# lam loaded as one row, the set-up reordered, and the first weight slice gated on the second q pair

## Chip, cores and metric

One core of one Trainium2 chip. The metric is device time of one execution in microseconds (us); the kernel before is given by the median of 11 executions.

## What is computed

Two steps. The first is a causal linear attention with decay over q, k and v of shape (4 batches, 8 heads, 768 positions, 64), cut into blocks of 64 in the reference; `lam` holds one decay factor per head (8 numbers in all). The second takes its output as 3072 tokens of 512 and runs them through two weight matrices with an activation between them.

```
per block, per batch and head:
  intra = ((qb @ kb.T) * Dmask) @ vb            # Dmask[i,j] = lam**(i-j) for i >= j, else 0
  inter = (qb * lam**(pos+1)) @ kv_state
  out   = intra + inter
  kv_state = lam**64 * kv_state + (kb * lam**(63-pos)).T @ vb
x = out as (tokens, heads*dim)                   # 3072 x 512
h = x @ w_in                                     # 512 -> 2048
g = h where h >= 1, 0 where h <= -1, else (h+1)**2 / 4
y = g @ w_out                                    # 2048 -> 512, float32
```

## The kernel before

**Tiling.** The attention runs over 24 chunks of 128 positions (6 to a batch). Powers of `lam` are put into q and k by elementwise products with tables, so a chunk needs only a triangular mask, not the full decay matrix. The feed-forward runs over 6 stages of 512 tokens, so four chunks of attention feed one stage. Chunks 0 and 1 are loaded as a pair in an even/odd layout (`PF = (0,)`), and take their own paths (`f_sp`, `f_op`).

**One chunk.** q, k and v are loaded in float32 by SyncE (SP). VectorE or GpSimd multiplies q and k by the tables and casts them to bf16 (`cast_q` L289, `cast` L284); ScalarE casts v into a block layout `vi` whose other half must be zero (L320). TensorE transposes q and k (L332, L325), which VectorE or ScalarE copy to SBUF (`kT` L342, `kbd` L335 for chunks 2 and 3, `qT` L338). TensorE then makes the scores (L390 for the first pair, L380 for chunks 2 and 3, L398 later), VectorE masks them (L405, L408, L410), TensorE adds the state's product and the scores' product with v into `po` (L425, L428; L440, L446 for the first pair) and updates the state in PSUM (L365, L369), from which ScalarE copies the diagonal blocks into `ubd` (L373). ScalarE copies `po` to `xT` (L458). The zero halves of `vi`, `kbd` and `ubd` are written once, in the set-up.

**Feed-forward.** `xT` times `w_in` (L470), ScalarE's relu (L479), three VectorE steps (L489, L495, L500), `gT` times `w_out` (L518), a ScalarE copy (L523), a store. `w_in` and `w_out` come in four slices each, through GpSimd's DMA queue with a cast to bf16 (L188, L192).

**Set-up (L105 to L156).** ScalarE loads its function table and issues the load of `lam` as a broadcast to all 128 partitions. GpSimd makes an identity matrix, two tables of positions (`pos_i`), and two masks, and zeroes two of the four `vi`; VectorE zeroes the other buffers. ScalarE takes Ln of `lam`, VectorE multiplies it by the positions (`arg`), and ScalarE's Exp of that gives `tab_q`, `tab_p` and `tab_k`.

**What sets the order.** Scheduling is manual: a planner written into the kernel (`run_plan`, L217) runs a small list simulation with a time for each operation, a due time worked back from TensorE's later work, and a model of the loads (`FIRST_BYTE` L212, L256 to L262), and then emits the operations in the order of the simulated starts. Each engine executes its own operations in that order, and waits in it. So the numbers of the model change the order of the program and nothing else. The loads and weight slices follow `ORDER` (L67): chunks 0 to 3, the four w_in slices, chunk 4, two w_out slices, chunk 5, two w_out slices, then chunks 6 and up. `LORD` gives the order of q, k and v (0, 1, 2) within a chunk. `GATE` (L72) makes a load or slice wait for the landing of another; without an entry, a chunk behind slices waits for the last slice but one, and the first w_out slice behind chunk 4 waits for the last w_in slice. `W_AFTER` (L215) puts slices behind the second q pair's casts on GpSimd. A load that waits holds all later loads on SP; a slice that waits holds GpSimd's later casts.

Of the kernel before, what the change touches and what calls it, by code (L numbers as in the profile page):

```python
# [8 lines left out]
F32 = mybir.dt.float32  # L9
# [14 lines left out]
def kernel(  # L24
# [44 lines left out]
    D0 = (8350, 11900, 15450, 19000)  # L69
    FIRST = [(0, 2), (2, 4)]  # L70
    L0 = [(0, 0), (0, 1), (1, 0), (1, 1), (0, 2), (1, 2), (0, 3), (1, 3)]
    GATE = {(0, 0): ("ld", 2, 1)}  # L72
    LORD = {0: (0, 1, 2), 2: (1, 0, 2)}
    DBG = False

    const = ctx.enter_context(tc.tile_pool(name="const", bufs=1))
# [26 lines left out]
    SYNC = mybir.DependencyInfo(mybir.DependencyClass.Sync, mybir.DependencyReason.DATA)  # L103

    nc.scalar.preload_act_table_set("natural_log_exp_and_others")  # L105
    lam_b = const.tile([128, H], F32)
    nc.scalar.dma_start(out=lam_b, in_=lam.partition_broadcast(128))


    ident = const.tile([128, 128], BF16)  # L110
    make_identity(nc, ident)
    pos_i = const.tile([128, 2, NCB], I32)
    nc.gpsimd.iota(pos_i[:, 0], pattern=[[C, NCB]], base=-S // 2, channel_multiplier=1)
    nc.gpsimd.iota(pos_i[:, 1], pattern=[[1, 2], [2 * C, NCB // 2]], base=-S // 2, channel_multiplier=2)
    causal = const.tile([128, 128], F32)
    nc.gpsimd.memset(causal, 1.0)
    nc.gpsimd.affine_select(
        out=causal, in_=causal, compare_op=AX.is_ge, fill=0.0,
        base=0, pattern=[[1, 2], [2, 64]], channel_multiplier=-1)
    causal2 = const.tile([128, 2, 128], F32)  # L120
    nc.gpsimd.memset(causal2, 1.0)
    for e in range(2):
        for rows, base in ((slice(0, 128), 128 - e), (slice(0, 64), -e)):
            nc.gpsimd.affine_select(
                out=causal2[rows, e], in_=causal2[rows, e], compare_op=AX.is_ge, fill=0.0,
                base=base, pattern=[[1, 2], [2, 64]], channel_multiplier=-2)


    NKB, NUB, NV = 3 if len(PF) < 2 else 0, 3, 4
    kbd = [const.tile([128, HP, 2, 128], BF16, name=f"kbd{i}") for i in range(NKB)]  # L130
    ubd = [const.tile([128, HP, 128], BF16, name=f"ubd{i}") for i in range(NUB)]
    vi = [const.tile([128, HP, 2, 2, D], BF16, name=f"vi{i}") for i in range(NV)]
    one = const.tile([128, 1], F32)
    nc.vector.memset(one, 1.0)
    for t in vi[:2] + kbd[:2] + ubd[:1]:
        nc.vector.memset(t, 0.0)
    for t in vi[2:]:
        nc.gpsimd.memset(t, 0.0)
    pos = const.tile([128, 2, NCB], F32)
    nc.scalar.copy(pos, pos_i)  # L140
    for t in kbd[2:] + ubd[1:]:
        nc.vector.memset(t, 0.0)
    ln_lam = const.tile([128, H], F32)
    nc.scalar.activation(out=ln_lam, in_=lam_b, func=AF.Ln)
    arg = const.tile([128, 2, NCB, H], F32)
    nc.vector.tensor_tensor(arg.rearrange("p a c h -> p (a c) h"), _bc(pos.rearrange("p a c -> p (a c)"), 2, H),
                            _bc(ln_lam, 1, 2 * NCB), op=AX.mult)
    tab_q = const.tile([128, 2, NCB // 2, H], F32)
    nc.scalar.activation(out=tab_q.rearrange("p a c h -> p (a c) h"), in_=arg[:, 1], func=AF.Exp)
    tab_p = const.tile([128, 2, 2, H], F32)  # L150
# [1 line left out]
                         in_=arg[:, 1].rearrange("p (e m) h -> p e (m h)", e=2)[:, :, :2 * H], func=AF.Exp, scale=-1.0)  # L152
    tab_k = const.tile([128, NCB, H], F32)
    nc.scalar.activation(out=tab_k, in_=arg[:, 0], func=AF.Exp, scale=-1.0)
    tab_qn = const.tile([128, NCB, H], F32)
    causal_n = const.tile([128, 128], F32)  # L156

# [51 lines left out]
        ops.append(OPS[key])  # L209

    MMS, FETCH = {"s": 8, "o": 12}, 1300
    FIRST_BYTE = 2950  # L212
    LDD, QXD, KXD, STD = 20000, 7000, 7000, 3000
    ON_POOL, ON_DVE = (1,), ((0, 1),)
    W_AFTER = {1: ("cq", 1, 1), 2: ("cq", 1, 1)}  # L215

    def run_plan(free):  # L217

        users = {x.key: [] for x in ops}
        for x in ops:  # L220
            x.needs = [OPS[y] for y in x.keys if y in OPS]
            for y in x.needs:
                users[y.key].append(x)
        left = {x.key: len(x.needs) for x in ops}
        topo = [x for x in ops if not x.needs]
        for x in topo:
            for u in users[x.key]:
                left[u.key] -= 1
                if left[u.key] == 0:
                    topo.append(u)  # L230
        assert len(topo) == len(ops)
        for x in reversed(topo):
            d = [u.due - u.ns - x.extra - LAT for u in users[x.key] if not u.dma]
            x.due = min(d + ([x.own] if x.own is not None else []), default=1e9)
            if x.dma or x.key[0] in ("l1", "l2"):
                x.due = x.own
        left = {x.key: len(x.needs) for x in ops}
        ready = {e: [] for e in free}
        for x in topo:
            if not x.needs:  # L240
                ready[x.eng].append((0, x))
        out_seq, xfer, dma_free, fetched = [], [0] * RING, FIRST_BYTE, 0
        while len(out_seq) < len(ops):
            t, e = min((max(free[e], min(r for r, _ in lst), xfer[-RING] if e == "SP" else 0), e)
                       for e, lst in ready.items() if lst)
            r, x = min(((r, x) for r, x in ready[e] if r <= t), key=lambda p: (p[1].due, p[0]))
            ready[e].remove((r, x))
            ns = x.ns + (720 if x.perf and free["POOL"] > t else 0)
            free[e] = t + ns
            x.t, x.end = t, t + ns + x.extra  # L250
            if e == "PE":
                n = fetched + 2 * MMS.get(x.key, MMS.get(x.key[0], 4))
                if n // 256 > fetched // 256:
                    dma_free = max(dma_free, t) + FETCH
                fetched = n
            if x.dma:  # L256
                dma_free = max(dma_free, t + (1300 if e == "SP" else 2100)) + x.dma
                x.end = dma_free + 1400
                if x.key[0] in ("ld", "lq") and x.key[1] >= (FAR if x.key[0] == "ld" else FAR // 2):
                    x.end += SLACK if (x.key[1] if x.key[0] == "ld" else 2 * x.key[1]) >= 10 else NEAR  # L260
                if e == "SP":
                    xfer.append(dma_free)  # L262
            out_seq.append((t, len(out_seq), x))
            for u in users[x.key]:
                left[u.key] -= 1
                if left[u.key] == 0:
                    ready[u.eng].append((max(y.t if y.eng == u.eng and y.key != u.gate else y.end + (XSL if u.eng == "SP" and y.eng == "POOL" and u.dma in (640, 1280) else LAT) for y in u.needs), u))
        for t, _, x in sorted(out_seq, key=lambda p: p[:2]):
            if DBG:
                print(f"{t / 1e3:9.3f} {x.due / 1e3:9.3f} {x.eng:5s} {x.ns:6.0f} {x.key}")  # L270
            x.fn()
# [83 lines left out]
    def last_of(a):  # L355

        return a | 1 if a // 2 in PF else a
# [257 lines left out]
    for it in order:  # L615
        if isinstance(it, tuple):
            prev = order[order.index(it) - 1]
            gated = GATE.get(it, len(w_seen) - 1 - prev % 2 if w_seen and isinstance(prev, int) else None)
            need = [("w",) + w_seen[-1], W_AFTER.get(len(w_seen))] if w_seen else []
            key = None  # L620
            if gated is not None:
                key = gated if isinstance(gated, tuple) else ("w",) + w_seen[gated]
                need.append(key)
            add(("w",) + it, "POOL", 900, lambda it=it, wait=gated: f_w(it, wait), need, due=pos_ * 1e-3,
                dma=2560)
            if key is not None:
                OPS[("w",) + it].gate = key
            w_seen.append(it)
            pos_ += 1
            continue  # L630
# [13 lines left out]
            pos_ += 1  # L644
        last_c = it

    for c in range(NCH):
        od, cb = o_due(c) - (DLEAD if c >= DX else 0), c % NCB
        lastu = c - 1 if cb else c - 2
# [28 lines left out]
        if CPS <= c < XT or pf:  # L678
            add(("kT", c), "DVE", 450, lambda c=c: f_kT(c), [("t", c), ("m", c - NQT, 1)])
        for hi in range(2 if c < CPS and not pf else 0):  # L680
            add(("kb", c, hi), "DVE", 365, lambda c=c, hi=hi: f_kb(c, hi), [("t", c), ("s", c - NKB, 1)])
        if cb < NCB - 1:
            add(("u", c), "PE", mm(*[128] * (8 if pf else 4)) + 100 * pf, lambda c=c: f_u(c),
                [("cast", last_of(c), 1), ("cast", last_of(c), 2), ("ub", lastu, 0), ("ub", lastu, 1), ("u", lastu)], due=od - 4000, extra=FILL)
            for hi in range(2):
                add(("ub", c, hi), "ACT", 372, lambda c=c, hi=hi: f_ub(c, hi), [("u", c), ("o", last_of(c - NUB + 1))])
        if pf:
            add(("s", c, 0), "PE", mm(*[128] * 4) + 250, lambda c=c: f_sp(c),
                [("kT", c), ("qT", m, 0), ("qT", m, 1), ("m", c - 2, 0), ("m", c - 2, 1), ("m", c - 1, 0), ("x", 1) if c == 3 else None], due=od - 2500, extra=FILL)
# [7 lines left out]
            add(("m", c, h), "DVE", 690, lambda c=c, h=h: f_m(c, h), [("s", c, h if c < CPS and not pf else 0), ("o", last_of(c - 3)), ("m", c, 0) if h else None])  # L697
        if pf:
            if c % 2:
                add(("o", c), "PE", mm(*[128] * (20 if c == 1 else 24)) + 250, lambda m=m: f_op(m),  # L700
                    [("m", c, 1), ("cast", c, 2), ("ub", c - 1, 0), ("ub", c - 1, 1), ("ub", c - 2, 0), ("ub", c - 2, 1),
                     ("x", c - 3), ("x", c - 2), ("kT", c), ("m", c - 1, 1)], due=od, extra=FILL)
        else:
# [54 lines left out]
            add(("y", y), "ACT", 600, lambda a=(s, ms): f_y(*a), [("l2", n2), ("y", y - 1), ("st", y - NO)])  # L758
            add(("st", y), "SP", 550, lambda a=(s, ms): f_st(*a), [("y", y), ("st", y - 1)], due=st_due(y), dma=780)

    run_plan({"PE": 5500, "ACT": 5600, "DVE": 5000, "POOL": 5000, "SP": 800})


# [28 lines left out]
```

## Time and profile before

| | us |
|---|---|
| median of 11 executions | 221.49 (219.71 to 222.27) |
| the profiled execution | 220.75 |
| its span | 219.0 |
| TensorE matmuls busy | 203.4 |
| first matmul | 8.07 |
| first matmul with w_in | 20.49 |
| first matmul with w_out | 37.56 |

The profile is of one execution; its times count from the start of the span. PE is TensorE, DVE VectorE, ACT ScalarE, POOL GpSimd; a row that begins with time, duration, engine and line is from the timeline, and the bracket at its end says how long the engine had been idle and what released it. SPq, ACTq and POOLq rows are the issue of a DMA, not its transfer. In the DMA view, q1 carries the loads that SP issues, q10 the one of ScalarE (`lam`), and q0 the weight slices of GpSimd.

### The profile page before, as it was taken

How to read it: one execution, taken by the hardware profiler on the slowest of the kernel's cores; microseconds unless marked ns; L12 is line 12 of the kernel's file. 1: busy time of each engine (PE TensorE's matmuls, PEld its weight loads, DVE VectorE, ACT ScalarE, POOL GpSimd, SP SyncE). 2: the span in 40 equal slices, each digit the busy share in tenths (PEclk: the TensorE clock that was granted, in tenths of full speed). 3: DMA queues.
4: the chain of work that ended last, by engine and by line, in shares of the span. 5: the costliest groups of instructions: out<-in, count | busy, mean ns of one | idle time of the engine just before them, and what ended most of it. 6: DMA issues, size and time to landing. Idle time of an engine off the chain costs nothing.

```text
span 219.0 us, 4453 instructions
## 1 busy us (share of the span) xinstructions
PE 203.4 (93%) x1776; PEld 132.9 (61%) x1800; DVE 137.3 (63%) x216; ACT 122.9 (56%) x220; POOL 63.0 (29%) x71
## 2 busy tenths in 40 slices
PE   0399799999999999999999999999999999999994
PEld 0278688685747977777766676744545444444442
DVE  6384588779544697979855967631697655554301
ACT  3347678454836757576648667545765534455030
POOL 8571094227524242812322800342100000000000
PEclk9999999999999999999999999999999999999998
DMA  4999999999999999999999727989785211110122
GB/s 111 278 223 217 200 224 200 185 226 233 157 226 140 243 156 226 168 192 230 200 236 186 151 48 157 198 196 218 245 147 168 62 37 48 48 48 0 51 96 96
DMA packets 96116, 35.42 MB, mean 162 GB/s; under 512 B 78560, under 2 KB 93152, under 8 KB 96096
## 3 DMA queue, kind: packets, MB, share of 16 engines
q1 hardware_dynamic: 91728, 30.94, 67.5%
q0 software_dynamic: 4224, 4.19, 11.8%
q8 instruction: 14, 0.23, 0.4%
q14 instruction: 6, 0.05, 0.1%
q10 hardware_dynamic: 144, 0.00, 0.0%
HBM read 27.27 MB, written 6.29 MB: 153 GB/s over the span
## 4 chain that ended last, share of the span: by engine, by line
PE 91%; DMA 3%; ACT 2%; issue 1%; DVE 1%; POOL 1%; POOLq 0%
PE ph L470 39%; PE py L518 36%; PE ps L398 3%; PE po L428 3%; DMA x0f<-in_q_dram 3%; PE pu L369 2%; PE py L512 1%; PE po L425 1%; PE pt L325 1%; PE py L332 1%; PE pu L365 1%; PE po L420 1%; PE po L446 1%; ACT xT L458 1%; PE po L417 1%
## 5 line engine op out<-in xcount | busy, mean ns | idle before, releaser
L470 PE MATMUL ph<-xT,w_in_sb 128*128 128x256 bf16 (+2 forms) x763 | 95.7, 272 | 1.7 <-ACT xT L458 1.2
L479 ACT ACTIVATE r<-ph,one 128x512 bf16<-128x512 f32 x96 | 65.9, 688 | 48.8 <-PE ph L470 31.9
L518 PE MATMUL py<-w_out_sb,gT 128*128 128x512 bf16 x349 | 86.5, 379 | 1.2 <-issue 0.3
L470 PEld LDWEIGHTS <-w_in_sb 128*128 128x128 bf16 x768 | 63.3, 98 | 24.7 <-issue 1.9
L518 PEld LDWEIGHTS <-gT 128*128 128x128 bf16 x368 | 34.8, 98 | 34.8
L489 DVE TENSOR_SCALAR t<-r 128x1024 bf16<-128x1024 bf16 x48 | 24.4, 509 | 39.6 <-ACT r L479 39.6
L495 DVE TENSOR_TENSOR w<-r,t 128x1024 bf16<-128x1024 bf16 x48 | 38.3, 799 | 1.5
L500 DVE TENSOR_TENSOR gT<-w,t 128x1024 bf16<-128x1024 bf16 x48 | 36.8, 766 | 1.5
L287 POOL TENSOR_TENSOR ks<-x1f,tab_k 128x512 bf16<-128x512 f32 x20 | 23.5, 1175 | 33.3 <-DMA x1f<-in_k_dram 20.7
L523 ACT COPY osb<-py 128x512 f32<-128x512 f32 x23 | 13.5, 585 | 17.9 <-PE py L518 16.6
L296 POOL TENSOR_TENSOR qs<-x0f,tab_q 128x512 bf16<-128x512 f32 x15 | 17.8, 1203 | 18.0 <-DMA x0f<-in_q_dram 13.3
L373 ACT CAST ubd<-pu 64x256 bf16<-64x256 f32 x40 | 14.6, 364 | 6.8 <-PE pu L369 3.7
L294 POOL TENSOR_TENSOR qs<-x0f,tab_qn 128x512 bf16<-128x512 f32 x8 | 9.3, 1161 | 27.1 <-DMA x0f<-in_q_dram 23.6
L410 DVE TENSOR_TENSOR sc<-ps,causal 128x512 bf16<-128x512 f32 x12 | 8.2, 686 | 9.0 <-PE pt L398 8.9
L458 ACT CAST xT<-po 128x512 bf16<-128x512 f32 x15 | 8.8, 584 | 8.3 <-PE po L428 5.1
L428 PE MATMUL po<-sc,vi 128*128 128x128 bf16 x112 | 10.5, 219 | 0.0
L332 PE MATMUL py<-ident,qs 128*128 128x128 bf16 x16 | 2.4, 306 | 8.7 <-POOL qs L296 8.1
L428 PEld LDWEIGHTS <-vi 128*128 128x128 bf16 x112 | 8.4, 98 | 1.0
L425 PE MATMUL po<-qT,ubd 128*128 128x128 bf16 x48 | 8.7, 219 | 0.0
L410 DVE TENSOR_TENSOR sc<-ps,causal_n 128x512 bf16<-128x512 f32 x8 | 5.5, 690 | 5.0 <-PE pt L398 5.0
L320 ACT CAST vi<-x2f 128x512 bf16<-128x512 f32 x14 | 8.5, 615 | 0.0
L410 DVE TENSOR_TENSOR sc<-pt,causal 128x512 bf16<-128x512 f32 x12 | 8.2, 680 | 0.0
(84 smaller groups left out, 132.1 us busy)
## 6 DMA issues: line engine op xcount, KB each, us to landing
out_dram<-osb SPq DMA_DIRECT2D x23, 256.0 KB, 2.5
x1f<-in_k_dram SPq DMA_DIRECT2D x22, 256.0 KB, 4.8
x2f<-in_v_dram SPq DMA_DIRECT2D x22, 256.0 KB, 5.0
x0f<-in_q_dram SPq DMA_DIRECT2D x8, 512.0 KB, 5.4
w_in_sb<-in_moe_w_in_dram POOLq DMA_DIRECT2D x4, 512.0 KB, 7.7
w_out_sb<-in_moe_w_out_dram POOLq DMA_DIRECT2D x4, 512.0 KB, 8.5
x0f<-in_q_dram SPq DMA_DIRECT2D x8, 256.0 KB, 4.1
raw<-in_k_dram SPq DMA_DIRECT2D x1, 512.0 KB, 6.8
```

Source lines behind the costliest of these rows:

```text
L287: eng.tensor_tensor(ks[c], qkv_ld[c, 1], _bc(tab, 2, D), op=AX.mult)
L296: eng.tensor_tensor(qs[m, e], qkv_ld[m, 0][:, :, e], _bc(tab_q[:, e, m % (NCB // 2), :], 2, D), op=AX.mult)
L373: nc.scalar.copy(out=ubd[c % NUB][HD[hi], :, HD[hi]], in_=pu[0][HD[hi], :, HD[hi]])
L410: nc.vector.tensor_tensor(sc_sb[c][:, g], pst[c, g], _bc(causal if c < DX else causal_n, 1, HP), op=AX.mult)
L428: nc.tensor.matmul(po[:, hp], lhsT=vi[c % NV][:, hp, hi].rearrange("p a d -> p (a d)"), rhs=sc_sb[c][:, hi, hp, :], start=(cb == 0 and hi ...
L470: nc.tensor.matmul(ph[:, j * m:(j + 1) * m], lhsT=w_in_sb[:, ko, (ni + j) * 128:(ni + j + 1) * 128], rhs=xT[s][:, ko, tok], start=(ko == 0 ...
L479: nc.scalar.activation(out=o, in_=x, func=AF.Relu, bias=one[:, 0:1])
L489: nc.vector.tensor_scalar(t, r, 0.5, 1.0, op0=AX.mult, op1=AX.min)
L495: nc.vector.tensor_tensor(w, r, t, op=AX.subtract)
L500: nc.vector.tensor_tensor(gT[s][:, f - RW * n:f, tok].rearrange("p (a b) m -> p a b m", a=RW), w.rearrange("p a (b m) -> p a b m", m=m), t ...
L518: nc.tensor.matmul(py_t[s, ms], lhsT=gT[s][:, ko, ms * 128:(ms + 1) * 128], rhs=w_out_sb[:, ko, :], start=(ko == 0), stop=(ko == FO - 1))
L523: nc.scalar.copy(out=osb[s, ms], in_=py_t[s, ms])
```

## The change

`lam` is loaded as one row of 8 numbers into one partition. Ln is taken there; the result is split into three bf16 pieces by VectorE (five operations on 1x8), and TensorE multiplies a row of ones by each piece and adds them up in PSUM (three matmuls), which gives the logarithm on all partitions. GpSimd makes the positions first. Two of the four `vi` are zeroed by ScalarE copies of zeroed ones. `kbd` has two buffers instead of three; they and the third `ubd` are zeroed by planned VectorE operations ("z") after chunk 0's k cast.

In the order of loads, chunk 2 takes q, k, v instead of k, q, v; the first w_in slice waits for the second q pair's landing instead of chunk 2's k; chunk 4's loads wait for the second w_in slice instead of the third, and chunk 6's for the second w_out slice instead of the third. The third slice's own tie to the q casts is dropped (it stays behind the second slice, which has it). The planner's model of loads and of some costs takes other numbers.

```diff
-    GATE = {(0, 0): ("ld", 2, 1)}
-    LORD = {0: (0, 1, 2), 2: (1, 0, 2)}
+    GATE = {(0, 0): ("lq", 1), 4: 1, 6: 5}
+    LORD = {0: (0, 1, 2), 2: (0, 1, 2)}
...
-    lam_b = const.tile([128, H], F32)
-    nc.scalar.dma_start(out=lam_b, in_=lam.partition_broadcast(128))
-    ident = const.tile([128, 128], BF16)
-    make_identity(nc, ident)
+    lam_r = const.tile([1, H], F32)
+    nc.scalar.dma_start(out=lam_r, in_=lam.rearrange("(o h) -> o h", o=1))
     pos_i = const.tile([128, 2, NCB], I32)
...
+    ident = const.tile([128, 128], BF16)
+    make_identity(nc, ident)
...
-    NKB, NUB, NV = 3 if len(PF) < 2 else 0, 3, 4
+    NKB, NUB, NV = 2, 3, 4
...
-    for t in vi[:2] + kbd[:2] + ubd[:1]:
+    ones = const.tile([1, 128], BF16)
+    nc.vector.memset(ones, 1.0)
+    for t in vi[:2]:
         nc.vector.memset(t, 0.0)
-    for t in vi[2:]:
-        nc.gpsimd.memset(t, 0.0)
+    rest = const.tile([1, 3, H], F32)
+    nc.scalar.activation(out=rest[:, 0], in_=lam_r, func=AF.Ln)
     pos = const.tile([128, 2, NCB], F32)
     nc.scalar.copy(pos, pos_i)
-    for t in kbd[2:] + ubd[1:]:
-        nc.vector.memset(t, 0.0)
-    ln_lam = const.tile([128, H], F32)
-    nc.scalar.activation(out=ln_lam, in_=lam_b, func=AF.Ln)
+    piece = const.tile([1, 3, H], BF16)
+    for i in range(3):
+        nc.vector.tensor_copy(piece[:, i], rest[:, i])
+        if i < 2:
+            nc.vector.tensor_tensor(rest[:, i + 1], rest[:, i], piece[:, i], op=AX.subtract)
+    ln_ps = pp_s.tile([128, HP, 128], F32, name="ps", tag="ps")
+    ln_lam = ln_ps[:, 0, :H]
+    for i in range(3):
+        nc.tensor.matmul(ln_lam, lhsT=ones, rhs=piece[:, i], start=(i == 0), stop=(i == 2))
+    nc.scalar.copy(vi[2], vi[0])
     arg = const.tile([128, 2, NCB, H], F32)
...
+    for t in ubd[:2]:
+        nc.vector.memset(t, 0.0)
...
+    nc.scalar.copy(vi[3], vi[1])
...
-    FIRST_BYTE = 2950
+    FIRST_BYTE = 2350
...
-    W_AFTER = {1: ("cq", 1, 1), 2: ("cq", 1, 1)}
+    W_AFTER = {1: ("cq", 1, 1)}
...
-                x.end = dma_free + 1400
+                x.end = dma_free + (400 if x.key[0] in ("ld", "lq") and x.key[1] < (CPS if x.key[0] == "ld" else CPS // 2) else 1000 if x.key[:2] == ("w", 0) else 1400)
...
-            need = [("w",) + w_seen[-1], W_AFTER.get(len(w_seen))] if w_seen else []
+            need = [("w",) + w_seen[-1] if w_seen else None, W_AFTER.get(len(w_seen))]
...
+    for i, t in enumerate(kbd + ubd[2:]):
+        add(("z", i), "DVE", 500 if i < NKB else 270, lambda t=t: nc.vector.memset(t, 0.0), [("cast", 0, 1)], due=12000)
...
-                add(("o", c), "PE", mm(*[128] * (20 if c == 1 else 24)) + 250, lambda m=m: f_op(m),
+                add(("o", c), "PE", mm(*[128] * (36 if c == 1 else 40)) + 60, lambda m=m: f_op(m),
...
-    run_plan({"PE": 5500, "ACT": 5600, "DVE": 5000, "POOL": 5000, "SP": 800})
+    run_plan({"PE": 4000, "ACT": 5600, "DVE": 4500, "POOL": 4300, "SP": 800})
```

The lines left out reorder the masks and add the "z" operations to the needs of the first users of `kbd` and `ubd`.

More of the change, by code (lines that the diff above doesn't have):

```diff
@@ L114 @@
     nc.gpsimd.iota(pos_i[:, 1], pattern=[[1, 2], [2 * C, NCB // 2]], base=-S // 2, channel_multiplier=2)
[L115 to L119, printed above, removed]
+    ident = const.tile([128, 128], BF16)
+    make_identity(nc, ident)
     causal2 = const.tile([128, 2, 128], F32)
@@ L126 @@
                 base=base, pattern=[[1, 2], [2, 64]], channel_multiplier=-2)
-    NKB, NUB, NV = 3 if len(PF) < 2 else 0, 3, 4
+    causal = const.tile([128, 128], F32)
+    nc.gpsimd.memset(causal, 1.0)
+    nc.gpsimd.affine_select(
+        out=causal, in_=causal, compare_op=AX.is_ge, fill=0.0,
+        base=0, pattern=[[1, 2], [2, 64]], channel_multiplier=-1)
+    NKB, NUB, NV = 2, 3, 4
     kbd = [const.tile([128, HP, 2, 128], BF16, name=f"kbd{i}") for i in range(NKB)]
@@ L680 @@
         for hi in range(2 if c < CPS and not pf else 0):
-            add(("kb", c, hi), "DVE", 365, lambda c=c, hi=hi: f_kb(c, hi), [("t", c), ("s", c - NKB, 1)])
+            add(("kb", c, hi), "DVE", 365, lambda c=c, hi=hi: f_kb(c, hi), [("t", c), ("s", c - NKB, 1), ("z", c % NKB)])
         if cb < NCB - 1:
@@ L685 @@
             for hi in range(2):
-                add(("ub", c, hi), "ACT", 372, lambda c=c, hi=hi: f_ub(c, hi), [("u", c), ("o", last_of(c - NUB + 1))])
+                add(("ub", c, hi), "ACT", 372, lambda c=c, hi=hi: f_ub(c, hi), [("u", c), ("o", last_of(c - NUB + 1)), ("z", NKB) if c == 2 else None])
         if pf:
```

## The prediction

> **What bounds the kernel now.** I read the page first. TensorE is busy 203.4 of 219.0 us. The row of slices shows where the other 15.6 us lie: nothing in the first slice, little in the second, part of the last.
>
> ```profile
> PE 203.4 (93%) x1776; PEld 132.9 (61%) x1800; DVE 137.3 (63%) x216; ACT 122.9 (56%) x220; POOL 63.0 (29%) x71
> ...
> PE   0399799999999999999999999999999999999994
> ```
>
> The table of stretches, summed, gives 8.75 us of idle TensorE before 10 us (8.07 of it before the first matmul), 2.3 us from 10 to 50 us, 1.3 us from 50 to 200 us and 3.2 us after that. The change touches only the set-up and the order of the early loads, so its gain has to come from the first 50 us. The chain that ended last, cut to 0 to 12 us, says what the 8.07 us are:
>
> ```profile
> 0.81 5.52 DMA x0f<-in_q_dram
> ...
> 6.47 1.56 POOL qs L296
> 8.03 0.05 issue
> 8.07 0.62 PE py L332 x4
> ```
>
> The first q pair lands at 0.81 + 5.52 = 6.33 us, GpSimd casts it, TensorE starts. The tables are not on this path: in the timeline they end before the load does.
>
> ```profile
> 4.61 0.21 ACT L144 ACTIVATE ln_lam<-lam_b 128x8 f32<-128x8 f32 x1 [2.32 <-DMA lam_b<-in_lam_dram]
> 4.86 0.26 DVE L146 TENSOR_TENSOR arg<-pos,ln_lam 128x96 f32<-128x96 f32 x1 [0.37 <-ACT ln_lam L144]
> 5.15 0.24 ACT L149 ACTIVATE tab_q<-arg 128x48 f32<-128x48 f32 x1 [0.33 <-DVE arg L146]
> ```
>
> tab_q is there at 5.39 us, 0.94 us ahead of the q pair. Earlier tables alone would bring nothing; what matters is whether lam's load holds up the q load. I took the DMA view in two windows: 2.5 to 4.5 us (lam's broadcast on q10, the q pair on q1), then 25.5 to 27.5 us, where the third q pair restarts q1 after a rest and no lam is about.
>
> ```profile
> q1 hardware_dynamic: 531, 0.27, 53.6%
> q10 hardware_dynamic: 107, 0.00, 2.4%
> ...
> q1 hardware_dynamic: 807, 0.41, 73.2%
> q0 software_dynamic: 29, 0.02, 7.7%
> ```
>
> The columns are packets, MB and share. lam's 144 packets run from about 1.8 to 4.5 us; in those two first microseconds q1 moves 0.27 MB, and 0.41 MB where lam is absent. The first q1 packet comes about 1.7 us after its issue (0.81 to about 2.53) against about 0.95 us (24.52 to 25.47). The whole 512 KB load took 5.5 us against 4.4.
>
> **A rule against this.** The Trainium skill ("DMA: Bandwidth & Descriptors", section "Anatomy of one DMA — SWDGE (gpsimd) path") puts the size-dependent part of its DMA fit at bytes over 436 GB/s; for lam's 4 KB that is an estimated 0.01 us, so shrinking it would gain nothing. The rows show 144 small packets lasting 2.7 us beside a slowed q1, so I count packets: the gain is 5.52 - 4.40 = 1.12 us. The bounds are 0 (the slow start belongs to the start of the program) and 1.9 us: at q1's full 334 GB/s from the first packet, 512 KB take 1.6 us, and with 1.0 us ahead and 1.0 behind the load would end at 4.4 instead of 6.33 us. I take 1.1, the one measured load of the same shape.
>
> **Part by part.**
>
> *Tables in one row.* lam's single packet should land soon after 1.8 us; the table load ends at 2.08, so Ln starts at 2.1 to 2.5. From 2.5: Ln 0.21 (row L144); five tiny DVE operations, between 0.06 (the memset of 128x1) and 0.26 (arg) each, so 0.3 to 1.3; three matmuls, nearest row four transposes in 0.61, so 0.5; arg 0.26; tab_q 0.24; some 0.3 of hand-over. tab_q ends at 4.3 to 5.3 us; I take 4.5, since eight elements are nearer to the memset. The new landing is 6.33 - 1.12 = 5.21. So it is hidden; at the slow end it costs up to 0.1. TensorE and its PSUM tile are idle then.
>
> *Zero-fills.* GpSimd loses 1.83 us of fills it did before 5.43. ScalarE gains two copies of 128x1024; nearest row L320, 0.62 for 128x512, so some 1.15 each: one while the pieces are made, one after tab_k, ended by 6 us; ScalarE's next work was at 8.72 (7.6 when shifted). Hidden. VectorE puts two kbd fills and one ubd fill (0.5 + 0.5 + 0.27 = 1.27 us) behind its k cast; there it stood idle 1.47 us (8.93 to 10.40, releaser the transposes), so they fit by 0.2. GpSimd's cast beside them, 1.03 us alone and 1.55 beside one DVE operation, may stretch to 2.5, and its transposes have 1.6 us of slack (9.83 to 11.46). Cost 0; if the plan puts a fill ahead of kT, 0.5.
>
> *First w_in slice and load order.* The second q pair becomes SP's fourth load instead of its fifth; the k of chunk 2 falls behind it. Before, k landed at about 11.4 and q at 13.0. Swapped and shifted by 1.1, q lands at about 10.5 (raw v's landing, 9.95 - 1.1, and 1.65 for 512 KB), k at 12.0. On GpSimd the slice waits for q; queued behind it are the two q casts and the other slices. The casts wait for the same load, so they pay the issue alone, 0.93 us. The slice itself, issued at 10.5 instead of 11.46, lands 6.4 us later at 16.9 and is first used at 20.49 - 1.1; the casts start at 11.5 instead of 13.08, and slices two to four go out from 13.6 instead of 15.11. Cast k of chunk 2 (12.58 before) now has its data at 12.0. None of these is a stall of TensorE before: from 10.88 to 20.1 us it works through its queue. Their value is slack: 0.
>
> *Chunks 4 and 6 sooner.* The loads of chunk 4 go from the third slice's landing (24.52) to the second's. The four slices took 6.4, 6.8, 8.6 and 10.4 us from issue to landing (the second from the median of four, 7.7), so the second landed at 15.11 + 6.8 = 21.9; shifted, 20.8. From there 1.05 MB of q, k, v share the engines with slices three and four at some 205 GB/s. Before, 0.74 MB of slices were left at 21.9 (205 GB/s until their bulk ended at 25.5); about 0.2 of that goes in the microsecond before the q packets come, and 0.55 to 0.6 at half of 205 GB/s take some 5.7 us. With the 1.5 us from the bulk's end to the last landing (25.5 to 27.0) the fourth slice lands at about 20.8 + 1.0 + 5.7 + 1.5 = 29.0; TensorE needs it near 34.82 - 1.1. GpSimd issues the first w_out slice on that landing, so 29.0 instead of 27.30; with 6.4 us (its time before) it lands at 35.4, needed at 37.56 - 1.1 = 36.4. Hidden by 1.0 us, where it had 3.9. Chunk 6 moves from 41.87 to about 36, beside slices that are needed from about 48. Both q, k, v groups were not what TensorE waited for, so the benefit is 0 too.
>
> *The waits in 23 to 28 us.* Two stalls stand here, 0.56 and 0.67 us, both on the xT copies of chunks 2 and 3.
>
> ```profile
> 24.19 0.92 PE L470 MATMUL ph<-xT,w_in_sb 128*128 128x256 bf16 x7 [0.56 <-ACT xT L458]
> ...
> 27.33 7.43 PE L470 MATMUL ph<-xT,w_in_sb 128*128 128x256 bf16 x64 [0.67 <-ACT xT L458]
> ```
>
> Only another order of TensorE's queue removes them. The plan, given earlier landings, may place chunks 2 and 3 sooner, and their q comes 1.4 us earlier than the common shift. Bounds: -1.2 and +0.6; I take -0.3, near nothing, since no data wait precedes them.
>
> **The clock.** Four transposes take 0.61 us until 19.5 us and 0.40 from 20.26, while the granted clock reads 1.00 throughout. The Trainium skill ("TensorE: Matmul & The Clock Gate", Part 1) says that the array runs at half rate until one busy window of about 3.4 us has passed, and that this window runs free. The end moves by half the start's shift plus half the switch's. If the switch goes along (as the row would have it), 1.1 us of start are 1.1 us of time. If it stays, only 0.55; if it comes one window sooner, (1.1 + 3.4) / 2 = 2.25. Its mean over executions is again 1.1, which I keep; the eleven times before spread by 2.6 us.
>
> **Sum.** Against the profiled execution (220.75 us; span 219.0 and 1.75 around it): 220.75 - 1.1 - 0.3 = 219.35. The median before is 0.74 above it, so 221.49 - 1.4 = 220.1 us.
>
> **Rivals.**
>
> *lam is not the brake.* For it: even the restart at 25.5 ramps for over a microsecond, so a ramp is the queue's own. Against: 1.7 against 0.95 us to the first packet. Then 0 to 0.4 us are gained: 221.3 us. Chance 0.20.
>
> *More comes through.* The q pair lands near 4.6, tables permitting (1.7 us earlier), and the stalls shrink by 0.6: 219.2 us. For it: full rate is reached within half a microsecond once lam's packets are gone. Against: the restart's 4.4 us. Chance 0.20.
>
> *w_out comes late (the slower one).* Chunk 4's loads push slice four, and GpSimd's wait for it holds back the first w_out slice. If that lands after 36.4 us TensorE waits at its first use of w_out; the gain is gone at 37.8 and the kernel is slower than 0.5% beyond 38.9. With the second slice's 9.3 us from issue to landing instead of 6.4, and GpSimd's two q casts (2.76 us) put ahead of the issue, it lands at 29.0 + 2.8 + 9.3 = 41.1, a loss of 4.7 us: 220.1 + 4.7 = 224.8 us. Against: in the trace nearly 4 us of slack. Chance 0.10.
>
> *Forecast:* chance 0.50, own range 219.4 to 220.9.
>
> **How the numbers follow.** A measurement of this kernel tells about 0.5% (1.1 us) from no change, so faster means below 220.38. The forecast stands 0.3 under it: 0.34 of its 0.50 is faster, 0.16 the same. The second rival is faster (0.20), the first the same (0.19) or, by a hair, slower (0.01); of the third 0.08 is slower, 0.02 the same. Faster 0.54, same 0.37, slower 0.09. The range takes the forecast, most of the second rival and the first: 218.8 to 221.6.
>
> **What would show it.** Right: lam's queue with a handful of packets; the first q packet near 1.8 us; the q pair landed near 5.2; the first matmul from the transposes near 7.0; tab_q before 5.2; VectorE's fills inside its wait for the first kT; the first w_in matmul near 19.3; the first w_out matmul without a wait. Wrong: the q pair still landing after 6 us, a TensorE wait on a w_in or w_out load between 30 and 40 us, or a start moved by a microsecond and an unmoved end.

## The result, and the profile after

The changed kernel takes 219.08 us (median of 12 executions, 218.51 to 220.06); the kernel before took 221.66 (median of 47, 219.71 to 223.04). The ratio is 0.9895 with a 95% interval of 0.9873 to 0.9917: about 2.3 us faster, where the forecast was 1.4 (220.1). The time lies below the forecast's own range (219.4 to 220.9) and next to the 219.2 of the second rival, "more comes through". The profiled executions are 218.63 and 220.75 us long, 2.1 apart, and their spans 216.9 and 219.0.

The page of the changed kernel, same rows as before: TensorE's busy time is almost what it was, so most of what went is idle time: 1.8 of the 2.1 us between the spans. In the row of slices the difference is in the first five.

```profile
PE 203.1 (94%) x1779; PEld 132.5 (61%) x1803; DVE 140.1 (65%) x221; ACT 124.5 (57%) x222; POOL 60.7 (28%) x69
...
PE   0589899999999999999999999999999999999994
```

The chain that ended last, cut to 0 to 12 us. The path is the same (load, GpSimd's cast, transposes); the load takes 4.26 us instead of 5.52, and all behind it comes 1.25 us sooner.

```profile
0.81 4.26 DMA x0f<-in_q_dram
...
5.22 1.55 POOL qs L307
6.77 0.04 issue
6.82 0.62 PE py L343 x4
```

The timeline of the tables: Ln starts at once behind the table load, and tab_q is there at 4.30 us, well ahead of the q pair at 5.07. The five small VectorE operations took 0.15 to 0.30 each.

```profile
2.10 0.21 ACT L140 ACTIVATE rest<-lam_r 1x8 f32<-1x8 f32 x1
...
3.77 0.26 DVE L154 TENSOR_TENSOR arg<-pos,ps 128x96 f32<-128x96 f32 x1 [0.33 <-PE ps L151]
...
4.06 0.24 ACT L159 ACTIVATE tab_q<-arg 128x48 f32<-128x48 f32 x1 [0.72 <-DVE arg L154]
```

The DMA view from 2.5 to 4.5 us (packets, MB, share): q1 moves 0.57 MB in the two microseconds in which it moved 0.27 beside lam's broadcast, and its first packets come between 1.8 and 2 us, as forecast. Queue q10 has two packets in the whole execution.

```profile
q1 hardware_dynamic: 1120, 0.57, 100.4%
```

Of the two waits on xT copies around 25 us, one is gone and the other is where it was, 2.26 us sooner. But three new waits stand before it in TensorE's timeline, between 12 and 19 us; they add up to 0.72 us. A wait of 0.16 us for `kbd`, at 20.26 us before, is gone too, so the waits listed between the first transposes and 30 us come to 2.58 us in both profiles.

```profile
12.62 1.01 PE L376 MATMUL pu<-vi,ks 64*128 64x128 bf16 x8 [0.27 <-ACT ubd L384]
...
14.46 0.61 PE L336 MATMUL pt<-ident,ks 128*128 128x128 bf16 x4 [0.29 <-DVE ks L298]
...
18.59 1.03 PE L481 MATMUL ph<-xT,w_in_sb 128*128 128x256 bf16 x8 [0.16 <-ACT xT L469]
...
25.07 7.43 PE L481 MATMUL ph<-xT,w_in_sb 128*128 128x256 bf16 x64 [0.67 <-ACT xT L469]
```

The second of them waits for VectorE's cast of chunk 2's k. That k had landed (4.96 us issue, 6.8 to landing: 11.8 us), but the plan puts the cast behind a mask, and there it starts beside GpSimd's q casts and takes 1.34 us; in the run with the old load order and the new set-up it stood ahead of them and took 0.68. In all eight profiles in which this cast starts beside GpSimd's, it ends 0.55 to 0.57 us behind them, however long that makes it (0.71 to 2.05 us). The rows are of the changed kernel, then of that run (set-up alone, below).

```profile
11.79 2.05 POOL L307 TENSOR_TENSOR qs<-x0f,tab_q 128x512 bf16<-128x512 f32 x2
...
13.06 1.34 DVE L298 TENSOR_TENSOR ks<-x1f,tab_k 128x512 bf16<-128x512 f32 x1
...
11.50 0.68 DVE L298 TENSOR_TENSOR ks<-x1f,tab_k 128x512 bf16<-128x512 f32 x1
```

In these two executions the array's switch to full rate (four 128-column matmuls in 0.4 us instead of 0.6) moved further than the start: from 20.0 to 16.9 us, in the midst of the first pair's output matmuls. Two rows of before, then two of after:

```profile
19.11 0.61 PE L380 MATMUL ps<-qT,kbd 128*128 128x128 bf16 x4
...
20.26 0.40 PE L380 MATMUL pt<-qT,kbd 128*128 128x128 bf16 x4 [0.16 <-DVE kbd L335]
...
16.79 0.31 PE L457 MATMUL po<-sc,vi 64*128 64x128 bf16 x1
...
16.99 0.22 PE L457 MATMUL po<-sc,vi 64*128 64x128 bf16 x1
```

### The profile page after: what moved, and what is told of

Same layout as the page of the kernel before. It is cut to its first block, busy times and chain, and to the rows that moved or that the text cites. A ratio compares the mean times of both kernels' runs of the same rounds, so it can differ in the third digit from the quotient of the medians.

```text
span 216.9 us, 4470 instructions
## 1 busy us (share of the span) xinstructions
PE 203.1 (94%) x1779; PEld 132.5 (61%) x1803; DVE 140.1 (65%) x221; ACT 124.5 (57%) x222; POOL 60.7 (28%) x69
## 4 chain that ended last, share of the span: by engine, by line
PE 91%; ACT 2%; DMA 2%; issue 2%; DVE 1%; POOL 1%; DVEq 0%; POOLq 0%
PE ph L481 39%; PE py L529 36%; PE po L439 3%; PE ps L409 3%; DMA x0f<-in_q_dram 2%; PE pu L380 2%; PE po L436 1%; PE py L523 1%; PE po L431 1%; ACT xT L469 1%; PE pt L336 1%; PE py L343 1%; PE po L428 1%; POOL qs L307 1%; PE po L457 1%
## 5 line engine op out<-in xcount | busy, mean ns | idle before, releaser
L500 DVE TENSOR_SCALAR t<-r 128x1024 bf16<-128x1024 bf16 x48 | 23.0, 479 | 35.0 <-ACT r L490 34.9
L506 DVE TENSOR_TENSOR w<-r,t 128x1024 bf16<-128x1024 bf16 x48 | 39.7, 826 | 1.4
L511 DVE TENSOR_TENSOR gT<-w,t 128x1024 bf16<-128x1024 bf16 x48 | 38.5, 803 | 1.7
L305 POOL TENSOR_TENSOR qs<-x0f,tab_qn 128x512 bf16<-128x512 f32 x8 | 8.8, 1099 | 26.1 <-DMA x0f<-in_q_dram 22.2
L439 PE MATMUL po<-sc,vi 128*128 128x128 bf16 x112 | 10.5, 219 | 0.0
L409 PE MATMUL ps<-qT,kT 64*128 64x128 bf16 x80 | 7.9, 219 | 0.0
```

The lines of the kernel that those rows point to most:

```text
L409: nc.tensor.matmul(pst[c, hi][:, hp, :], lhsT=kT[c][HD[hi], hp, :], rhs=q_cols(c, hp, HD[hi]), start=True, stop=True)
L439: nc.tensor.matmul(po[:, hp], lhsT=vi[c % NV][:, hp, hi].rearrange("p a d -> p (a d)"), rhs=sc_sb[c][:, hi, hp, :], start=(cb == 0 and hi ...
L500: nc.vector.tensor_scalar(t, r, 0.5, 1.0, op0=AX.mult, op1=AX.min)
L506: nc.vector.tensor_tensor(w, r, t, op=AX.subtract)
L511: nc.vector.tensor_tensor(gT[s][:, f - RW * n:f, tok].rearrange("p (a b) m -> p a b m", a=RW), w.rearrange("p a (b m) -> p a b m", m=m), t ...
```

## Experiments

All times are medians; "before" is the kernel before on the same chip. Its median was 220.56 us on the chip of the old load order with new numbers and of the two kernels with added matmuls, and 221.4 to 221.95 on the others, so a difference of a few tenths between kernels from two chips says little.

**Set-up alone, order alone.** The first takes the changed kernel and puts the load order, the gates and the planner's numbers back; the second takes those alone on the old set-up.

```diff
 (set-up alone: the changed kernel with)
+    GATE = {(0, 0): ("ld", 2, 1)}
+    LORD = {0: (0, 1, 2), 2: (1, 0, 2)}
+    FIRST_BYTE = 2950
+    W_AFTER = {1: ("cq", 1, 1), 2: ("cq", 1, 1)}
...
+                x.end = dma_free + 1400
...
+            need = [("w",) + w_seen[-1], W_AFTER.get(len(w_seen))] if w_seen else []
...
+                add(("o", c), "PE", mm(*[128] * (20 if c == 1 else 24)) + 250, lambda m=m: f_op(m),
...
+    run_plan({"PE": 5500, "ACT": 5600, "DVE": 5000, "POOL": 5000, "SP": 800})
 (order alone: the kernel before with the changed kernel's lines of these)
```

> The changed set-up alone (lam as one row, Ln spread by three matmuls, zero-fills moved), with the load order, the gates and the planner's numbers of before; TensorE's order is that of before. Theory (lam's small packets hold up the first q load): the q pair lands near 5.1 us instead of 6.33, the first transposes start near 6.8, and the time is 1.3 us below before (about 220.3). Rival (the gain comes from the load order and the planner's new order): the time is within 0.4 us of before. Rival (the start moves, but the array's clock switch does not): 0.6 us below before.

Measured: 219.72 us against 221.4, ratio 0.9933 (0.9911 to 0.9955). The q pair landed at 5.25, the transposes started at 6.99 us, the switch of the clock was at 19.3. The theory's 1.3 us lie in the interval (1.0 to 2.0 us); the rivals' 0.4 and 0.6 do not. So the set-up brings 1.5 us of the 2.3. The wait for `ubd` stands here too, with the old load order.

```profile
0.81 4.44 DMA x0f<-in_q_dram
...
6.99 0.62 PE py L343 x4
...
12.79 1.01 PE L376 MATMUL pu<-vi,ks 64*128 64x128 bf16 x8 [0.27 <-ACT ubd L384]
```

> The changed load order, gates and planner's numbers alone, on the set-up of before. Theory: the q pair still lands near 6.3 us and the first transposes start near 8.1; the second q pair is earlier but TensorE works through its queue at that point, so the time is 0 to 0.5 us below before. Rival (the order is what gains): 1.0 us or more below before.

Measured: 222.85 against 221.4, ratio 1.0073 (1.0043 to 1.0103): slower, which neither case expected. In the profile TensorE has three waits of 0.27, 0.22 and 0.39 us between 14 and 21 us, and lam landed late. Three rows of the timeline, then two of the chain that ended last:

```profile
6.40 0.21 ACT L144 ACTIVATE ln_lam<-lam_b 128x8 f32<-128x8 f32 x1 [4.11 <-DMA lam_b<-in_lam_dram]
...
6.94 0.24 ACT L149 ACTIVATE tab_q<-arg 128x48 f32<-128x48 f32 x1 [0.33 <-DVE arg L146]
...
7.42 1.55 POOL L296 TENSOR_TENSOR qs<-x0f,tab_q 128x512 bf16<-128x512 f32 x1 [1.98 <-ACT tab_p L151]
...
0.81 6.46 DMA x0f<-in_q_dram
...
7.42 1.55 POOL qs L296
```

The bracket of GpSimd's first cast names ScalarE's `tab_p`, but the cast reads `tab_q`, which was ready at 7.18 us. The q pair landed at 7.27, and the cast follows 0.15 us later, as it followed 0.14 us behind the landing in the kernel before. So the load bounds the start here too, with the tables only 0.09 us ahead of it, and the transposes started at 9.02 us. The load is late because its packets led (13 of them before 2 us, none of lam's) and lam's then rode beside them. From 3.5 to 4 us:

```profile
q1 hardware_dynamic: 87, 0.04, 29.5%
q10 hardware_dynamic: 21, 0.00, 1.9%
```

**lam's broadcast put back.** Behind the one row, unused:

```diff
     nc.scalar.dma_start(out=lam_r, in_=lam.rearrange("(o h) -> o h", o=1))
+    lam_b = const.tile([128, H], F32)
+    nc.scalar.dma_start(out=lam_b, in_=lam.partition_broadcast(128))
```

> The changed kernel with a second, unused load of lam put back behind the one row: the broadcast to 128 partitions of before. The tables stay early; only its packets return. Theory: the q pair lands 0.8 to 1.2 us later than in the changed kernel (near 6.0), and the time is about 1.2 us above the changed kernel. Rival (the broadcast's packets cost nothing; what made the start earlier is the set-up's other work): the landing stays at 5.1 us and the time does not move.

Measured: 220.66 us, ratio to before 0.9976 (0.9958 to 0.9994), 1.6 us above the changed kernel. The landing of q did not move (its cast starts at 5.12), so the theory missed the place; nearly all its packets were through before the broadcast began. The load behind it paid: raw k's cast starts at 8.42 instead of 7.01.

```profile
5.12 1.54 POOL L309 TENSOR_TENSOR qs<-x0f,tab_q 128x512 bf16<-128x512 f32 x1 [1.34 <-DMA x0f<-in_q_dram]
...
8.42 1.55 POOL L300 TENSOR_TENSOR ks<-raw,tab_p 128x512 bf16<-128x512 f32 x1 [1.75 <-DMA raw<-in_k_dram]
```

The DMA view of this kernel from 3.5 to 4 us, before the broadcast's packets, and from 4.5 to 5, beside them:

```profile
q1 hardware_dynamic: 339, 0.17, 114.4%
...
q1 hardware_dynamic: 74, 0.04, 29.1%
q10 hardware_dynamic: 32, 0.00, 2.9%
```

The load in flight beside these packets falls to a fifth of its rate in this half microsecond, and to 148 and 230 packets in the next two. That settles that these packets slow a load: but for this load and its issue on ScalarE, nothing differs between this kernel and the changed one. That in the kernel before the slowed load was the q pair's is shown by its DMA view and by the set-up alone, not by this run.

**Gates of chunks 4 and 6 put back** (`GATE = {(0, 0): ("lq", 1)}`).

> The changed kernel with chunks 4 and 6 gated as before (on the third w_in slice and the third w_out slice). Theory: TensorE waited for neither, so the time is within 0.3 us of the changed kernel. Rival (the sooner gates feed the later stages): 0.5 us or more above it. Rival (they cost something by delaying the weight slices): 0.3 us or more below it.

Measured: 219.21 us, ratio to before 0.9913 (0.9881 to 0.9945), 0.13 above the changed kernel. They bring nothing that can be measured.

**Old load order, new numbers** (the changed kernel with the old `GATE` and `LORD`).

> The changed kernel with the old load order for chunk 2 (k, q, v) and the old gates, but the new numbers in the planner's model. It parts what the set-up alone left (some 0.8 us to the changed kernel) between load order and planned order. If the planned order gains, the time is that of the changed kernel within 0.3 us (about 219.1). If it is the second q pair's place ahead of chunk 2's k, the time is that of the set-up alone (about 219.8), or above it where TensorE's new order meets q late.

Measured: 219.47 us, ratio to before 0.9944 (0.9925 to 0.9962). By the medians it lies between the two cases: 0.25 below the set-up alone, 0.39 above the changed kernel. By the ratio it stands with the set-up alone (0.9933), outside the changed kernel's interval. The two measures disagree, so this did not tell the cases apart.

**TensorE kept busy in its idle time.** 28 matmuls of the identity with itself, then in a second kernel also five and four in two gaps.

```diff
         nc.tensor.matmul(ln_lam, lhsT=ones, rhs=piece[:, i], start=(i == 0), stop=(i == 2))
+    def warm(n):
+        t = pp_h.tile([128, MS], F32, name="ph", tag="ph")
+        for i in range(n):
+            nc.tensor.matmul(t[:, :128], lhsT=ident, rhs=ident, start=True, stop=True)
+    warm(28)
 (second kernel, behind the q transposes of (0, 0) and the k transposes of chunk 0)
+            warm(5)
+            warm(4)
```

> The changed kernel with 28 matmuls of the identity with itself behind the three that spread Ln, into a tile that nobody reads: TensorE is busy from about 3.7 to 6.7 us, where it stood idle. Theory that the array's half rate ends with the busy window that it sees, and that every microsecond of earlier switch is worth half a microsecond: the switch comes before 14 us and the time falls by 1 us or more below the changed kernel, unless VectorE and ScalarE then bound the first chunks, when it falls by less than 0.7. Rival (the switch is bound to the dense work behind 15 us, and short early work does nothing): within 0.3 us of the changed kernel.

Measured: 218.88 us, ratio to before 0.9922 (0.9906 to 0.9938), 0.2 below the changed kernel by the median: the rival. The added 3.17 us of dense matmuls run on into the first transposes, 3.74 us in all (3.59 to 7.33), and did not switch the rate before the two gaps; the switch came at 18.3 us.

```profile
3.59 3.17 PE L155 MATMUL ph<-ident 128*128 128x128 bf16 x28
...
8.00 0.59 PE L348 MATMUL py<-ident,qs 128*128 128x128 bf16 x4 [0.67 <-ACT qT L354]
...
9.53 0.31 PE L406 MATMUL ps<-qT,kT 64*64 64x128 bf16 x1 [0.52 <-DVE kT L358]
```

> As the kernel with 28 idle-time matmuls, with five more behind the first q transposes and four behind the first k transposes, where TensorE stood idle 0.67 and 0.52 us. If gaps between 7 and 10 us keep the array at half rate or send it back there, this falls below the kernel with 28 by 0.5 us or more; if not, they are the same within 0.3 us.

Measured: 218.79 us, ratio 0.9924 (0.9901 to 0.9947), the same time, but not the same profile. Now the rate switches at 8.7 us:

```profile
8.38 0.61 PE L341 MATMUL pt<-ident,ks 128*128 128x128 bf16 x4
8.81 0.40 PE L155 MATMUL ph<-ident 128*128 128x128 bf16 x4
...
18.80 1.05 PE L490 MATMUL ph<-xT,w_in_sb 128*128 128x256 bf16 x8 [1.59 <-DMA w_in_sb<-in_moe_w_in_dram]
```

So filling the gaps of 0.67 and 0.52 us brought the switch forward; the next kernel, with the same matmuls added, switches early as well (near 9.2 us). But ten microseconds at full rate show no gain, because the first w_in matmul then waits for its slice: that landing is the next bound, 0.2 us behind the start that the changed kernel has.

**The first w_in slice sooner**, with those matmuls and without (`GATE = {(0, 0): ("ld", 0, 2), 4: 1, 6: 5}`, the landing of the first v).

> As the kernel with idle-time and gap-filling matmuls, whose first w_in matmul waited 1.59 us for its slice; here the first w_in slice is gated on the first v's landing (about 8.7 us) instead of the second q pair's. Theory (with the clock switched early, the slice's landing is the bound): the slice is issued near 8.7, the first w_in matmul comes before 18 us, and the time is 0.5 us or more below the changed kernel. Rival (the slice's transfer holds up q and k of chunk 2, so the wait only moves): within 0.3 us of the changed kernel.

Measured: 218.14 us against 221.81, ratio 0.9838 (0.98 to 0.9877); 0.9 below the changed kernel, and the fastest of all. The first w_in matmul starts at 16.04 us. Of the 2.6 us that it gains there on the changed kernel, 1.3 are given back at once, in a wait for chunk 3's k (VectorE's cast of it waited 1.38 us for the load and starts at 17.62 us, against 15.73 in the kernel with added matmuls and the slice behind q):

```profile
16.04 1.03 PE L490 MATMUL ph<-xT,w_in_sb 128*128 128x256 bf16 x8 [0.37 <-ACT xT L478]
...
17.62 0.69 DVE L303 TENSOR_TENSOR ks<-x1f,tab_k 128x512 bf16<-128x512 f32 x1 [1.38 <-DMA x1f<-in_k_dram]
...
18.37 0.40 PE L341 MATMUL pt<-ident,ks 128*128 128x128 bf16 x4 [1.30 <-DVE ks L303]
```

> The changed kernel with only the first w_in slice's gate put on the first v's landing, no added matmuls. Theory: without the early switch TensorE does not wait for the slice, so nothing is gained, and q's second pair comes later: 0 to 0.5 us above the changed kernel. Rival (the slice is the bound already): 0.4 us or more below it.

Measured: 219.1 us, ratio 0.9876 (0.9842 to 0.991): that of the changed kernel, and 1.0 above the kernel with both, on the same chip. Neither the early clock nor the early slice shows a gain alone; each hides the other.

**The kernel before again, and parts of it.** No edit in the first; the planner's numbers alone in the second; order alone once more in the third.

> The kernel before once more, for a second profile of it: where lam lands (4.6 us in the first), where the q pair lands (6.33) and where four transposes change from 0.6 to 0.4 us (20 us). If lam's packets and the clock's switch vary from execution to execution, one of these moves by 0.5 us or more; the time lies in 219.7 to 223.0.

Measured: 221.26 us in one execution. lam landed at 4.93, the q pair at 6.68, transposes from 8.43, the switch at 19.5 us. So lam and the load came 0.3 us later than in the first profile of this kernel and the switch 0.5 sooner: all three vary.

> The kernel before with the planner's new numbers alone: old set-up, old load order, old gates. It asks why order and numbers together were 1.5 us slower on the old set-up, where lam landed at 6.4 us and the tables were late. If a 512 KB load in fourth place pushes lam's broadcast back, lam lands here at 4.6 to 5 us and the time is within 0.5 us of before; if lam's place varies by chance, or the planned order is the cause, the time is 1 us or more above before.

Measured: 221.7 against 221.81, ratio 0.9998 (0.998 to 1.0017). lam landed at 6.2 us here, with a 256 KB load in fourth place and the time of before. So lam can land late without a 512 KB load in that place. The chain again names the q pair (landed at 7.08 us, tab_q ready at 6.99), and the transposes started at 8.83.

> New load order, gates and numbers on the old set-up, a second time, for a second profile. In the first, lam landed at 6.4 us and the tables were ready only at 7.4; the kernel with the new numbers alone had the same late lam (6.2) and the time of before. If the 1.5 us come from lam's late landing, lam is at 6 us or later again and the first transposes start near 9.0; if lam lands before 5 us this time and the time is still 1 us above before, they come from the load order behind it.

Measured: 222.48 against 221.95, ratio 1.0027 (1.0008 to 1.0047). The same program as the order alone above, and lam landed early:

```profile
4.53 0.21 ACT L144 ACTIVATE ln_lam<-lam_b 128x8 f32<-128x8 f32 x1 [2.23 <-DMA lam_b<-in_lam_dram]
...
6.40 1.55 POOL L296 TENSOR_TENSOR qs<-x0f,tab_q 128x512 bf16<-128x512 f32 x1 [0.96 <-DMA x0f<-in_q_dram]
```

Two executions of one program, 1.9 us apart in lam's landing and 1.0 in TensorE's start. The broadcast's place between the loads changes from execution to execution. TensorE's waits of 0.27, 0.26 and 0.22 us (ending at 13.8, 15.6 and 19.7 us) are there again. These waits are what both profiles of the order alone have in common, and the new numbers with the old order do not have them. lam's place adds to the time of some executions, but with the old order too, so it cannot be charged to the new one.

## Why the prediction was right, and where its size was off

*What bounds the start.* Right: the q pair's load, not the tables. In all five profiles with the broadcast in front (the kernel before twice, its new numbers, the order alone twice) the chain that ended last begins with this load. Where lam landed late, the tables were ready only 0.09 us ahead of it, not the 0.94 of the forecast's profile. That lam's small packets slow the load beside them is shown by the broadcast put back. The byte count of the fit quoted from the Trainium skill (0.01 us, an estimate) is two orders below what the row of lam was worth.

*The size of that term.* Too small. The 1.12 us came from one execution of before. In those five profiles the q pair landed at 6.33, 6.68, 7.08, 7.27 and 6.26 us, and the transposes started at 8.07, 8.43, 8.83, 9.02 and 8.00, on average 8.47; in the set-up alone, the changed kernel and the ones with other gates or order they started at 6.99, 6.82, 6.73, 6.80 and 6.68, on average 6.80. That is 1.67 us instead of 1.1, and the profile that the forecast rested on was one of the early ones. It also had lam's packets first, which delays q's first packet; the two latest landings are those where q's packets came first and lam's rode beside them. A late first packet is therefore not the only way to lose this time. Part of before's spread may lie here (2.56 us over its first 11 executions, 1.55 over 12 of the changed kernel), but no run ties single times to the landing.

*Luck in the number.* The time is that of the second rival, but not for its reasons: the q pair landed at 5.07 us, not near 4.6, and the stalls did not shrink. A larger shift of the start, an earlier clock switch and a rest of unknown cause add up to it. The profiled pair itself (2.1 us) matches the branch that the prediction named, a switch one window sooner; since this switch varies by 3.3 us among kernels with the same start, that was chance.

*Tables.* 4.30 us measured, 4.5 said. ScalarE's copies took 1.03 and 1.04 (said 1.15) and lay hidden; VectorE's two kbd fills lay in its wait, the ubd fill behind kT; GpSimd's cast stayed at 1.55 us where 2.5 was feared. No cost, as said.

*First slice and load order.* The slice was issued at 10.84 (said 10.5) and landed at 17.4 (16.9). The order's value of 0 was right only in sum. The wait for chunk 2's k (0.29 us) comes with the new order, which brings GpSimd's q casts ahead of the k cast and holds it up; the one for `ubd` (0.27) comes with the new set-up too, since the set-up alone has it. The wait of 0.56 us at 24 us is gone only where the new set-up, load order and numbers meet. On the old set-up, where the plan keeps that wait, the order is a loss of 0.3 to 0.7%.

*Gates of 4 and 6.* Value 0, as said. The contention was overestimated: the fourth slice landed so that w_out could be issued at 26.88 (said 29.0), the first w_out slice was there at 32.8 (35.4), used at 35.30 without a wait. The slower rival would have had to use up 2.5 us of slack.

*The waits at 23 to 28 us.* Said 0.3 gained; in the profiled pair 0.56 and 0.16 are gone and 0.72 are new, so the term was worth nothing there. What stands between the set-up alone (0.9933) and the whole (0.9895) is some 0.8 us, with intervals that overlap. Old order with new numbers did not place it, so its cause stays open; a sooner clock switch (16.9 against 19.3 us in the two profiles) would make 1.2 us of the 1.5 that lie between these two at 25 us, but one profile each does not show that it is the rule.

*The clock.* The formula (half the start's shift plus half the switch's) gives (1.25 + 3.1) / 2 = 2.2 us for the profiled pair; the spans differ by 2.1. That the switch goes along with the start on average fits roughly: it came at 20.0, 19.5, 19.7, 19.3 and 18.8 us in the five profiles with the broadcast in front and at 19.3, 16.9, 19.5, 16.2 and 18.8 in the five without, on average 1.3 us sooner. With the 1.67 us of the start the formula gives an estimate of 1.5 us, what the set-up alone brought; but these are different programs, one profile each.

The Trainium skill ("TensorE: Matmul & The Clock Gate", Part 1) lets the window run free, and a switch that varies between 16.2 and 19.5 us among five kernels with the same start fits that. Its length of some 3.4 us does not fit: in the kernel before TensorE was busy from 10.88 to 20.0 us with no gap by the profile's count, which holds at least one whole window of that length, and the rate stayed at half. Two rows of the table of stretches (window, length, PE busy, then the other engines; the third number from the end is the granted clock):

```profile
10.88:16.00 5.12, 5.12 (x64) 3.80 (x64) 4.32 (x9) 2.27 (x7) 3.85 (x5) 1.00 1.24 226
...
15.00:20.00 5.00, 5.00 (x61) 4.45 (x60) 2.15 (x6) 4.00 (x9) 2.40 (x4) 1.00 1.24 214
```

The 3.74 us without a gap in the first kernel with added matmuls did not switch the rate, 5.1 us with one gap of 0.14 us in the second did. What sets the moment stays open.

## What to carry to other kernels

Count a load's packets, not its bytes: a few kilobytes in 128 pieces beside the first large load can cost more than a microsecond at the start, where TensorE has nothing else to do. Price a start from several profiled executions, because a small transfer can take its place early or late. When a bracket and the chain name different releasers, ask which tile the operation reads. And ask which landing comes next before an engine is made faster: here clock and weight slice had to be moved together.

## What the runs showed of the hardware

Beside 20 to 58 packets of 32 bytes per half microsecond from ScalarE's queue, SP's queue fell from about 340 packets of 512 bytes to between 74 and 230 (the kernel with the broadcast put back, 4 to 6 us). A ramp remains without them: in the changed kernel q1 moved 56 packets by 2.5 us and 106 from 2.5 to 3 us, before it reached 337 in half a microsecond. Two loads issued 0.02 us apart from two engines were served in either order, in two executions of one program: lam's packets first and landed at 4.5 us, or q's first and lam landed at 6.4. VectorE's k cast of 128x512 took 0.68 us ahead of GpSimd's casts; started beside them it took 0.71 to 2.05 us and ended 0.55 to 0.57 us behind them. In the kernel before the array ran at half rate through nine microseconds of busy TensorE (10.9 to 20.0 us), and the profile's granted clock read 1.00 all along.
